# Late modulation vectors as VectorE dot products over transposed w_mod columns, and a second full set of gate and up weight buffers, in an adaLN attention and SwiGLU block

## The chip, the cores and the metric

The kernel runs on one core of one Trainium2 chip. The metric is the device time of one execution in microseconds (us). A time here is the median of several executions. The profile is one execution, and its span (first to last instruction) is about 2 us shorter than the time of the same execution.

The names of the engines: PE is TensorE (matmuls), DVE is VectorE, ACT is ScalarE, POOL is GpSimd, SP is SyncE, which here only issues DMA. "SPq" in a line of the profile is SP's instruction queue.

## The reference

```python
mod = (silu(c) @ w_mod).reshape(1, 6, 1, 1024)       # c: 1 x 1024, w_mod: 1024 x 6144
sa, ca, ga, sb, cb, gb = (mod[:, i] for i in range(6))
h = layernorm(x) * (1 + ca) + sa                     # x: 2048 x 1024
x = x + ga * attention(h)     # 32 heads of 128, 4 KV heads, the last W = 512 of 2048 cached keys
h = layernorm(x) * (1 + cb) + sb
x = x + gb * ffn(h)           # silu(h @ w_gate) * (h @ w_up) @ w_down, width 3584
return x                      # all in bf16
```

The six modulation vectors of 1024 values come from one product of a vector with a matrix. Two of them (sa, ca) are needed at once. The other four are late: the gate ga is first needed when the first chunk of 512 tokens finishes attention, cb and sb when its second layernorm begins, and gb only in the feed-forward part.

## The kernel before

The kernel handles four chunks of 512 tokens. Attention is cut into 128 steps, one head of one chunk each. A step issues 4 score matmuls, 8 matmuls that make q for three steps ahead, from step 13 on 8 matmuls with wo, and 16 matmuls of probabilities with V. By the trace a step takes 3.50 us up to step 12 and 5.22 us from step 13 on, and nearly all of that is PE time. Other work is hung on the steps by `at(k, function, ...)`. After attention comes the feed-forward part (FFN) for all four chunks.

Three parts matter. First, nearly all loads go through one queue, that of SP. While the attention steps are emitted they are pinned in program order, so a load that waits for something holds up every load behind it:

```python
stage = {"dma": True, "steps": False}
def pin(ins, what="steps"):
    return tc.keep_in_program_order(ins) if stage[what] else ins
def fetch(out, in_):
    pin(nc.sync.dma_start(out=out, in_=in_), "dma")
def load_wq(cc, hg, parts=(0, 1)):                    # wq of four heads, in two halves
    for i in parts:
        t = blkB("wq", [P, 4, 512])
        load(t, wq_v[:, 4 * i:4 * i + 4, hg * 512:(hg + 1) * 512])     # load() is a fetch()
        wq_tiles[(cc, hg, i)] = t
...
for k in range(NU + 1):                               # the 128 attention steps
    if k % 4 >= 2 and 4 * (k // 4) + 8 < NU:
        g = 4 * (k // 4) + 8
        load_wq(g // H, (g % H) // 4, (k % 4 - 2,))   # e.g. steps 10, 11: wq first used in step 13
    if k < NU: emit_s(k)
    if k + LEAD < NU: emit_q(k + LEAD)                # LEAD = 3
    run_tasks(k)
    if k >= 1: emit_o(k - 1)
```

Second, the four late vectors. They are made as rows by matmuls with silu(c) as the stationary operand, stored to DRAM as rows, and come back: a gate as a broadcast to all 128 partitions, a column (cb, sb) by a gather of 4-byte values:

```python
def load_rows(vec, part):                             # 1 MB of w_mod, half of one vector's rows
    t = hpool.tile([P, 4, D], BF16, name="wmr", tag="hT")
    load(t, wm_v[:, 4 * part:4 * part + 4, vec * D:(vec + 1) * D])
def mod_rows(n, part):                                # 16 matmuls, four times
    ps = mm("row_ps")
    ...
    nc.tensor.matmul(ps[32 * i:32 * i + 32, :], lhsT=sil32[:, 4 * part + k, :], rhs=..., ...)
    ...
    fetch(out=row_d[n], in_=r[0:P:32, :])             # four rows of 512 fp32
def load_gate(n, k, dst):
    fetch(out=dst..., in_=row_d[n][k:k + 2, :].partition_broadcast(P))
def load_cols(n, k, dst, add_one):
    fetch(out=dst, in_=row_d[n][k:k + 2, :].rearrange("a (b p) -> p (a b)", p=P))
for n, vecs in enumerate(((2, 4), (5, 3))):           # (ga, cb) and (gb, sb)
    for part in range(2):
        k = 16 * n + 8 * part
        at(k, load_rows, vecs[0], part); at(k + 2, load_rows, vecs[1], part)
        at(k + 5, mod_rows, n, part)                  # steps 5, 13, 21, 29
    at(16 * n + 15, load_gate, n, 0, gb_bc if n else ga_bc)
    at(16 * n + 16, load_cols, n, 2, sb if n else cb1, n == 0)
```

Third, the weights of the FFN. Gate and up weights of four 128-wide feature tiles take four buffers of 512 KB. The pool `blkB` has seven, so two full sets (eight) do not fit:

```python
def load_gu(cc, fg):
    for nm, v in (("wg", wg_v), ("wu", wu_v)):
        for i in range(2):
            t = blkB(nm, [P, 4, 512])                 # pool blkB: bufs=7
            load(t, v[:, 4 * i:4 * i + 4, fg * 512:(fg + 1) * 512])
            gu_w[(cc, fg, nm, i)] = t
```

## Time and profile before

| what | before |
|---|---|
| time, median of the first 3 runs | 1285.66 us |
| span of the profiled execution | 1282.7 us |
| PE busy | 1269.7 us (99%) |
| DVE busy | 577.8 us (45%) |
| mean granted TensorE clock | 0.998 |

The first part of the page of the kernel before gives the span and, for each engine, busy time, share and number of instructions:

```profile
span 1282.7 us, 18139 instructions
...
PE 1269.7 (99%) x7601; PEld 642.9 (50%) x7601; DVE 577.8 (45%) x1271; ACT 333.9 (26%) x433; POOL 1.2 (0%) x8
```

PE is the limit: it has 13 us without work in the whole execution. What the change takes away has to be PE work, or one of these few holes. The groups view of the kernel before, restricted to the tile row_ps, shows the PE work in question. Its columns are line, engine, operation, tiles, shape, count, then busy us and mean ns of one, then idle before it:

```profile
L779 PE MATMUL row_ps<-wmr,sil 128*32 128x512 bf16 x64 | 4.2, 382 | 0.0
```

So 64 matmuls take 4.2 us of PE. The waits view of the kernel before shows the holes. A line names who waited, for what, the us in total, how often, and the longest. Here are two waits of PE:

```profile
PE gu_ps L1168 <- DMA wu<-in_B_w_up_dram: 2.1, 1, 2.1
...
PE a_ps L1096 <- DVE acc L1102: 0.7, 1, 0.7
```

And one of DVE, from the same view of that engine:

```profile
DVE modT L802 <- DMA modT<-row_d: 3.4, 1, 3.4
```

The second and the third line belong together: DVE stood 3.4 us on the columns gathered from row_d, an accumulator copy came late behind it, and PE lost 0.7 us. The first line is the only weight wait of the FFN. The timeline of SP around it shows its reason (start, duration, queue, line, operation, tiles, count):

```profile
743.56 6.84 SPq L848 DMA_TRANSPOSE hT<-xn  x4
750.50 0.53 SPq L664 DMA_DIRECT2D wu<-in_B_w_up_dram  x1
```

The timeline of PE shows its end; the square brackets hold the idle time before the instruction and what ended it:

```profile
754.79 1.04 PE L1168 MATMUL gu_ps<-hT,wu 128*128 128x512 bf16 x4 [2.10 <-DMA wu<-in_B_w_up_dram]
```

The wu tile could be issued only at 750.50 us, because its buffer came free late and four transposes, 6.84 us together, stood before it in the queue.

### The profile page before, as it was taken

To read this page: it belongs to the slowest core of one execution; us is meant where nothing else is said; L and a number is where in the kernel's file an instruction comes from. 1 tells how busy PE (TensorE), PEld (TensorE's weight loads), DVE (VectorE), ACT (ScalarE), POOL (GpSimd) and SP (SyncE) were. 2 spreads that over 40 slices of the span, in tenths; PEclk is the share of its full clock that TensorE was granted. 3 is DMA by queue.
4 is the path that set the end of the run, shared out by engine and by line. 5 is a ranking of instruction groups with operands and counts; after the bars stand their busy time and mean duration, and the time that the engine had idled before them with its cause. 6 is when DMAs were issued, how large, how long until landed. Compare 5 with 4: busy or idle time off the path is not lost.

```text
span 1282.7 us, 18139 instructions
## 1 busy us (share of the span) xinstructions
PE 1269.7 (99%) x7601; PEld 642.9 (50%) x7601; DVE 577.8 (45%) x1271; ACT 333.9 (26%) x433; POOL 1.2 (0%) x8
## 2 busy tenths in 40 slices
PE   8999999999999999999999999999999999999998
PEld 4555555555555555555554444444444444444444
DVE  4464467865577755576653642221212221221122
ACT  3543334333333433333341111011100111011100
POOL 0000000000000000000000000000000000000000
PEclk9999999999999999999999999999999999999999
DMA  9888476557355654445487484454536455454401
GB/s 293 269 204 232 152 154 167 141 149 195 91 129 155 144 148 140 123 142 131 132 207 221 142 234 150 140 189 147 181 102 216 143 165 164 135 193 134 146 21 48
DMA packets 280108, 204.21 MB, mean 159 GB/s; under 512 B 113865, under 2 KB 273609, under 8 KB 280018
## 3 DMA queue, kind: packets, MB, share of 16 engines
q1 hardware_dynamic: 275106, 198.78, 54.2%
q10 hardware_dynamic: 4912, 4.20, 1.0%
q8 instruction: 61, 1.00, 0.3%
q14 instruction: 29, 0.24, 0.1%
HBM read 174.08 MB, written 4.21 MB: 139 GB/s over the span
## 4 chain that ended last, share of the span: by engine, by line
PE 95%; DMA 2%; DVE 1%; SPq 1%; ACT 0%; issue 0%; DVEq 0%
PE gu_ps L1168 29%; PE a_ps L1096 17%; PE q_ps L1019 17%; PE d_ps L1188 15%; PE o_ps L1064 9%; PE s_ps L1032 8%; DMA wm<-in_w_mod_dram 1%; SPq L664 1%; DMA hT<-xn 0%; DMA modT<-row_d 0%; DMA wu<-in_B_w_up_dram 0%; PE row_ps L779 0%; PE q_ps L940 0%; DVE st L816 0%; SPq L848 0%; ACT pT L1034 0%
## 5 line engine op out<-in xcount | busy, mean ns | idle before, releaser
L1034 ACT ACTIVATE pT<-s_ps 128x1024 bf16<-128x1024 f32 x256 | 248.7, 1020 | 341.8 <-PE s_ps L1032 341.8
L1096 PE MATMUL a_ps<-wo,oT 128*128 128x512 bf16 x1024 | 241.9, 379 | 0.7 <-DVE acc L1102 0.7
L1019 PE MATMUL q_ps<-hT,wq 128*128 128x512 bf16 x1000 | 236.7, 379 | 0.3 <-DVE modT L755 0.3
L1168 PE MATMUL gu_ps<-hT,wu 128*128 128x512 bf16 x896 | 211.8, 379 | 2.1 <-DMA wu<-in_B_w_up_dram 2.1
L1168 PE MATMUL gu_ps<-hT,wg 128*128 128x512 bf16 x896 | 211.7, 379 | 0.0
L1174 DVE TENSOR_TENSOR guT<-gu_ps,sg 128x512 bf16<-128x512 f32 x112 | 77.4, 691 | 283.5 <-ACT sg L1173 283.5
L1173 ACT ACTIVATE sg<-gu_ps 128x512 bf16<-128x512 f32 x112 | 66.9, 597 | 490.9 <-PE gu_ps L1168 439.7
L1188 PE MATMUL d_ps<-wd,guT 128*128 128x512 bf16 (+2 forms) x952 | 194.2, 366 | 0.0
L916 DVE CAST qT<-q_ps 128x512 bf16<-128x512 f32 x128 | 88.3, 691 | 176.6 <-PE q_ps L1019 176.0
L1096 PEld LDWEIGHTS <-oT 128*128 128x128 bf16 x1024 | 99.9, 98 | 122.1 <-issue 1.9
L1019 PEld LDWEIGHTS <-wq 128*128 128x128 bf16 x1000 | 97.8, 98 | 117.8 <-issue 0.3
L1188 PEld LDWEIGHTS <-guT 128*128 128x128 bf16 x952 | 90.9, 98 | 102.9
L1064 PEld LDWEIGHTS <-pT 128*128 128x128 bf16 x2048 | 126.6, 98 | 30.6 <-issue 0.4
L1168 PEld LDWEIGHTS <-wu 128*128 128x128 bf16 x896 | 87.6, 98 | 108.1 <-DMA wu<-in_B_w_up_dram 2.6
L1168 PEld LDWEIGHTS <-wg 128*128 128x128 bf16 x896 | 87.7, 98 | 105.4
L1064 PE MATMUL o_ps<-v_sb,pT 128*128 128x130 bf16 x2048 | 137.1, 220 | 0.0
L1032 PE MATMUL s_ps<-qT,kT 128*128 128x512 bf16 x512 | 131.5, 379 | 0.6 <-ACT pT L1034 0.6
L1051 DVE TENSOR_TENSOR oq<-o_ps,rl 128x256 bf16<-128x256 f32 (+2 forms) x256 | 101.3, 420 | 4.3
L1192 DVE TENSOR_TENSOR f<-d_ps,gb_bc 128x512 f32<-128x512 f32 (+2 forms) x34 | 22.5, 661 | 147.0 <-PE d_ps L1188 147.0
L1104 DVE TENSOR_TENSOR acc<-a_ps,acc 128x512 f32<-128x512 f32 x64 | 44.1, 689 | 38.9 <-PE a_ps L1096 38.9
L1032 PEld LDWEIGHTS <-kT 128*128 128x128 bf16 x512 | 44.9, 98 | 31.7 <-issue 1.3
L816 DVE BATCH_NORM_STATS2 st<-x 128x6 f32<-128x512 bf16 x64 | 41.3, 680 | 2.9 <-DMA x<-in_A_x_dram 2.6
(75 smaller groups left out, 309.3 us busy)
## 6 DMA issues: line engine op xcount, KB each, us to landing
wq<-in_A_wq_dram SPq DMA_DIRECT2D x64, 512.0 KB, 4.1
wo<-in_A_wo_dram SPq DMA_DIRECT2D x64, 512.0 KB, 5.5
wg<-in_B_w_gate_dram SPq DMA_DIRECT2D x56, 512.0 KB, 5.1
wu<-in_B_w_up_dram SPq DMA_DIRECT2D x56, 512.0 KB, 3.8
wd<-in_B_w_down_dram SPq DMA_DIRECT2D x56, 512.0 KB, 6.4
wmr<-in_w_mod_dram SPq DMA_DIRECT2D x8, 1024.0 KB, 11.4
x<-in_A_x_dram SPq DMA_DIRECT2D x16, 256.0 KB, 5.7
wm<-in_w_mod_dram SPq DMA_DIRECT2D x4, 1024.0 KB, 10.5
```

The lines of the kernel that those rows point to most:

```text
L916: nc.vector.tensor_copy(out=t, in_=q_ps)
L1019: nc.tensor.matmul(q_ps, lhsT=wq_tiles[(cc, h // 4, dt // 4)][:, dt % 4, (h % 4) * P:(h % 4 + 1) * P], rhs=hT[("h1", cc)][:, dt, :], start ...
L1032: nc.tensor.matmul(s_ps[:, i, :], lhsT=kT[:, kv, j * P:(j + 1) * P], rhs=qT[g], start=True, stop=True)
L1034: nc.scalar.activation(out=p[:, 2 * jj:2 * jj + 2, :], in_=s_ps, func=ACT.Exp, scale=scale)
L1051: nc.vector.tensor_tensor(out=dst, in0=ps[:, s0:s0 + cnt, 0:Dh], in1=sc, op=ALU.mult)
L1064: nc.tensor.matmul(o_slot["ps"][:, s_, :], lhsT=pT[g][:, j, t * P:(t + 1) * P], rhs=v_sb[:, kv, j, 0:VN], start=(j == 0), stop=(j == WT - 1))
L1096: nc.tensor.matmul(a_ps, lhsT=oT[(cc, 2 * q + i)][:, hh % 4, t * P:(t + 1) * P], rhs=wo_tiles[(cc, q, dh, i)][:, hh % 4, :], start=(hh == ...
L1104: nc.vector.tensor_tensor(out=acc[(cc, t)][:, dsl], in0=a_ps, in1=acc[(cc, t)][:, dsl], op=ALU.add)
L1168: nc.tensor.matmul(ps[:, n, :], lhsT=gu_w[(cc, fg, nm, dt // 4)][:, dt % 4, fi * P:(fi + 1) * P], rhs=hT[("h2", cc)][:, dt, :], start=(dt ...
L1173: nc.scalar.activation(out=g, in_=ps[:, 0, :], func=ACT.Silu)
L1174: nc.vector.tensor_tensor(out=guT[(cc, fg)][:, fi, :], in0=ps[:, 1, :], in1=g, op=ALU.mult)
L1188: nc.tensor.matmul(d_ps, lhsT=guT[(cc, f // 4)][:, f % 4, t * P:(t + 1) * P], rhs=wd_tiles[(cc, dh, f // 4)][:, f % 4, c0:c0 + w], start=( ...
```

## The change

The intent is threefold. The four late vectors should cost PE nothing: w_mod is loaded transposed by DMA, so that a column of w_mod lies along the free axis of a partition, and DVE multiplies it with silu(c) (broadcast to all partitions) and sums. The result is a column, so cb and sb need no way through DRAM at all. Only the gates, which are needed as rows, go from columns to DRAM and back as a broadcast. And the eighth buffer for gate and up weights is put where V was, which is dead once attention is over.

```diff
-    def load_rows(vec, part): ...      # plain load, 1 MB
-    def mod_rows(n, part): ...         # 16 TensorE matmuls, rows to DRAM
-    def load_cols(n, k, dst, add_one): ...   # columns gathered from DRAM
+    def spread_c():
+        fetch(out=c_d, in_=sil_r)
+        fetch(out=c_bc.rearrange("p (a b) -> p a b", a=DT), in_=c_d.partition_broadcast(P))
+    def load_wmT(vec, part):
+        t = hpool.tile([P, 4, D], BF16, name="wmT", tag="hT")
+        for i in range(4):
+            c0 = vec * D + (4 * part + i) * P
+            pin(nc.sync.dma_start_transpose(out=t[:, i, :], in_=w_mod[:, c0:c0 + P]), "dma")
+    def mod_dot(vec, j, dst):
+        pin(nc.vector.scalar_tensor_tensor(out=junk, in0=t[:, j % 4, :], scalar=1.0, in1=c_bc,
+                                           op0=ALU.mult, op1=ALU.mult, accum_out=dst[:, j:j + 1]))
+    def store_gate(n):
+        d = dp.tile([DT, P], FP32, name="col_d", tag="col_d", bufs=2)
+        with nc.allow_non_contiguous_dma(reason="columns to 1024 values"):
+            fetch(out=d.rearrange("a p -> p a"), in_=mod_col[:, n, :])
+    def load_gate(n, dst):
+        fetch(out=dst.rearrange("p (a b) -> p a b", a=DT), in_=col_d[n].partition_broadcast(P))
 ...
+    at(0, spread_c)
+    for i, (vec, dst) in enumerate(((2, mod_col[:, 0, :]), (4, cb1), (3, sb), (5, mod_col[:, 1, :]))):
+        for part in range(2):
+            k = 1 + 8 * i + 4 * part
+            at(k, load_wmT, vec, part)
+            for j in range(4):
+                at(k + 3 + j, mod_dot, vec, 4 * part + j, dst)
+        k = 1 + 8 * i + 10
+        if vec == 4: at(k, add_one, cb1)
+        elif vec in (2, 5):
+            at(k + 1, store_gate, vec // 5)
+            at(k + 2, load_gate, vec // 5, gb_bc if vec == 5 else ga_bc)
 ...
+    v_blk = v_flat[:, 0:2048].rearrange("p (a b) -> p a b", a=4)          # in V's place
     def load_gu(cc, fg):
         for nm, v in (("wg", wg_v), ("wu", wu_v)):
             for i in range(2):
-                t = blkB(nm, [P, 4, 512])
+                spare = (cc * NFG + fg) % 2 == 1 and nm == "wu" and i == 1
+                t = v_blk if spare else blkB(nm, [P, 4, 512])
```

More of the change, by code (lines that the diff above doesn't have):

```diff
@@ L756, in mod_cols @@
                                 scalar1=1.0 if add_one else 0.0, scalar2=None, op0=ALU.add)
-    sil32 = const.tile([P, DT, 32], BF16, name="sil32")
-    for dt in range(DT):
-        nc.vector.tensor_scalar(out=sil32[:, dt, :], in0=ones_bf[:, 0:32],
-                                scalar1=siluc[:, dt:dt + 1], scalar2=None, op0=ALU.mult)
-    wm_rows = []
-    row_part = []
-    row_d = {}
-    def load_rows(vec, part):
-        t = hpool.tile([P, 4, D], BF16, name="wmr", tag="hT")
-        load(t, wm_v[:, 4 * part:4 * part + 4, vec * D:(vec + 1) * D])
-        wm_rows.append(t)
@@ L774, in mod_rows @@
-    def mod_rows(n, part):
-        ps = mm("row_ps")
-        tiles = [wm_rows.pop(0) for _ in range(2)]
-        for k in range(4):
-            for i in range(4):
-                nc.tensor.matmul(ps[32 * i:32 * i + 32, :], lhsT=sil32[:, 4 * part + k, :],
-                                 rhs=tiles[i // 2][:, k, (i % 2) * 512:(i % 2 + 1) * 512],
-                                 start=(k == 0), stop=(k == 3))
-        if part == 0:
-            r = blkC("row", [P, TCW], FP32)
-            nc.vector.tensor_copy(out=r, in_=ps)
-            row_part.append(r)
-        else:
-            r = row_part.pop()
-            nc.vector.tensor_tensor(out=r, in0=ps, in1=r, op=ALU.add)
-            d = dp.tile([4, TCW], FP32, name="row_d", tag="row_d", bufs=2)
-            fetch(out=d, in_=r[0:P:32, :])
-            row_d[n] = d
@@ L793, in load_gate @@
-    def load_gate(n, k, dst):
-        fetch(out=dst.rearrange("p (a b) -> p a b", a=2),
-                          in_=row_d[n][k:k + 2, :].partition_broadcast(P))
-    def load_cols(n, k, dst, add_one):
-        src = row_d[n][k:k + 2, :].rearrange("a (b p) -> p (a b)", p=P)
-        with nc.allow_non_contiguous_dma(reason="1024 values to columns"):
-            fetch(out=dst, in_=src)
-        if add_one:
-            nc.vector.tensor_scalar(out=dst, in0=dst, scalar1=1.0, scalar2=None, op0=ALU.add)
+    c_d = dp.tile([DT, P], BF16, name="c_d", tag="c_d", bufs=1)
@@ new lines, in fast_path @@
+    c_bc = const.tile([P, D], BF16, name="c_bc")
+    mod_col = const.tile([P, 2, DT], FP32, name="mod_col")
+    wm_cols = {}
+    col_d = {}
+    def spread_c():
[6 more added lines that the diff above has]
+            pin(nc.sync.dma_start_transpose(out=t[:, i, :], in_=w_mod[:, c0:c0 + P]), "dma")
+        wm_cols[(vec, part)] = t
@@ new lines, in mod_dot, with add_one @@
+    def mod_dot(vec, j, dst):
+        t = wm_cols[(vec, j // 4)]
+        junk = wk.tile([P, D], BF16, name="junk", tag="junk", bufs=1)
+        pin(nc.vector.scalar_tensor_tensor(out=junk, in0=t[:, j % 4, :], scalar=1.0, in1=c_bc,
+                                           op0=ALU.mult, op1=ALU.mult,
+                                           accum_out=dst[:, j:j + 1]))
+    def add_one(dst):
+        pin(nc.vector.tensor_scalar(out=dst, in0=dst, scalar1=1.0, scalar2=None, op0=ALU.add))
+    def store_gate(n):
+        d = dp.tile([DT, P], FP32, name="col_d", tag="col_d", bufs=2)
+        with nc.allow_non_contiguous_dma(reason="columns to 1024 values"):
+            fetch(out=d.rearrange("a p -> p a"), in_=mod_col[:, n, :])
+        col_d[n] = d
@@ L1111, in emit_wo @@
             nc.vector.tensor_tensor(out=x1, in0=f, in1=x1, op=ALU.add)
-    for n, vecs in enumerate(((2, 4), (5, 3))):
+    at(0, spread_c)
+    for i, (vec, dst) in enumerate(((2, mod_col[:, 0, :]), (4, cb1), (3, sb),
+                                    (5, mod_col[:, 1, :]))):
         for part in range(2):
-            k = 16 * n + 8 * part
-            at(k, load_rows, vecs[0], part)
-            at(k + 2, load_rows, vecs[1], part)
-            at(k + 5, mod_rows, n, part)
-        at(16 * n + 15, load_gate, n, 0, gb_bc if n else ga_bc)
-        at(16 * n + 16, load_cols, n, 2, sb if n else cb1, n == 0)
+            k = 1 + 8 * i + 4 * part
[3 more added lines that the diff above has]
+        k = 1 + 8 * i + 10
+        if vec == 4:
+            at(k, add_one, cb1)
+        elif vec in (2, 5):
+            at(k + 1, store_gate, vec // 5)
+            at(k + 2, load_gate, vec // 5, gb_bc if vec == 5 else ga_bc)
     for tt in range(QT, S // P):
@@ L1152, in fast_path @@
     wd_tiles = {}
+    v_flat = v_sb.rearrange("p a b c -> p (a b c)")
+    v_blk = v_flat[:, 0:2048].rearrange("p (a b) -> p a b", a=4)
     def load_gu(cc, fg):
```

## The prediction

> **What bounds the kernel now.** TensorE: the page shows PE busy 1269.7 of 1282.7 us (99%), clock 0.998. About half of the idle 13 us is the start, where the chain of waits ends on the first w_mod loads until 22 us; nothing changes there. DVE is busy 45%. So the change can only win TensorE time and the few holes in it.
>
> **What it removes, all on the critical path.**
> 1. The 64 row_ps matmuls: four bursts, 4.2 us busy (groups view); a step with a burst takes 4.58 instead of 3.50 us (timeline, score matmuls). -4.2 us.
> 2. The DVE wait for the columns loaded from row_d (waits view, 3.4 us), which held an accumulator copy back and left PE idle 0.73 us (step 6.12 instead of 5.22 us). They now come by a DVE sum. -0.8 us.
> 3. The hole at 752.7-754.8 us: gu_ps waited 2.1 us for a wu tile, issued only at 750.5 behind four hT transposes, because with seven buffers the eighth tile waits until its predecessor group is nearly done. With the spare buffer it goes out some 18 us earlier. -2.2 us. It is the only FFN weight wait in the waits view, so the second full set wins no more.
>
> Sum: -7.2 us.
>
> **What it adds.**
> - 32 dot products of 128x1024 on DVE. The same form (squares of wq) takes 1.215 us plus 0.08 us for the accumulator: about 40 us, in steps 4 to 36 (42 to 195 us). DVE is busy about 2 us per 3.5-us step there; a dot raises that to 3.0-3.2, and in steps 10-12, where layernorm adds about 1 us, over 3.5. From step 13 a step is 5.2 us. DVE runs in order and may free PSUM late: 1 to 3 us of PE idle in steps 8-16.
> - 32 DMA transposes of 256 KB for 8 plain loads of 1 MB. SyncE spends 1.25 us issuing an hT transpose, 0.5 us on a plain megabyte: 5 us per half vector, not 0.5. Four hT transposes moved 220 GB/s in their best 2 us (stretches view), plain loads 350. The Trainium skill ("DMA: Bandwidth & Descriptors", Latency and other measured facts) gives 261 GB/s, near this. So 2-3.5 us more DMA time per half, where the DMA share is already 0.8-1.0 up to 128 us, and the one in-order queue also carries wq, wo and oT. Followed step by step, wq still lands 2-5 us before its use: 0 to 2 us lost, before 110 us.
> - c through DRAM and column stores of 4-byte elements (about 5 us to land, like modT): hidden.
>
> **Prediction.** -7.2 + 2.5 = -4.7 us: 1281.0 us, 8 times in 10 between 1275.5 and 1290.0. Faster by over 2%: 0.01; within 2%: 0.95; slower by over 2%: 0.04.
>
> **What would show it.** Right: no row_ps; no gu_ps wait for wu; PE busy about 1265.5; FFN stages unchanged otherwise; DVE busy about 612 us, dots near 1.22 us; new PE idle only between 40 and 130 us, released by DVE (qT, oq, acc) or by wq or wo DMA. Wrong: PE idle after 200 us, or a wu wait elsewhere.
>
> **What would make it wrong.** Transposes straight from w_mod (256-byte rows, 12-KB pitch) far slower than those from SBUF, so that dots block DVE and DVE blocks PSUM by several us per half; or the SP queue falling behind, which adds up before step 13: then 15-30 us slower. If DVE absorbs the dots wholly: 1278.

## More of the kernel before

One more view of the kernel before is needed later, the timeline of SP in the early steps. It shows when wq was issued, and what stood before it:

```profile
51.61 0.81 SPq L664 DMA_DIRECT2D wq<-in_A_wq_dram  x1
52.52 1.31 SPq L664 DMA_DIRECT2D wmr<-in_w_mod_dram  x1
58.46 6.15 SPq L1081 DMA_TRANSPOSE oT<-oq  x4
64.66 0.58 SPq L664 DMA_DIRECT2D wq<-in_A_wq_dram  x1
...
77.40 0.45 SPq L664 DMA_DIRECT2D wq<-in_A_wq_dram  x1
...
84.50 0.53 SPq L664 DMA_DIRECT2D wq<-in_A_wq_dram  x1
```

The issues at 51.61 and 64.66 us are the two halves of the wq that step 13 uses first (step 13 began at 72.32 us), those at 77.40 and 84.50 us are for step 17 (it began at 95.19 us). One load of a megabyte of w_mod, at 52.52 us, holds the queue for 1.31 us. The queue runs 8 to 11 us ahead of the use.

## The result, and the profile after

| | before | after |
|---|---|---|
| time, median of the fast runs of the same rounds (6 each) | 1286.62 us | 1293.48 us |
| range | 1285.42 to 1288.03 | 1289.08 to 1294.75 |
| span of the profiled execution | 1282.7 us | 1291.7 us |
| PE busy | 1269.7 us | 1270.2 us |
| DVE busy | 577.8 us | 606.9 us |
| mean granted clock | 0.998 | 0.992 |

The ratio is 1.005, with a 95% interval of 1.0034 to 1.0066. A ratio here is the mean time of one kernel's fast runs over that of the other's of the same rounds, so it is not quite the ratio of the medians. The kernel became slower by 0.5%. That is within 2%, but it is outside the predicted range of 1275.5 to 1290.0 us, and the sign is wrong.

The first part of the page after:

```profile
span 1291.7 us, 18094 instructions
...
PE 1270.2 (98%) x7537; PEld 641.9 (50%) x7537; DVE 606.9 (47%) x1323; ACT 333.8 (26%) x433; POOL 1.2 (0%) x8
```

PE has 64 matmuls fewer and yet is busy 0.5 us longer, and its idle time grew from 13 to 21.5 us. The parts of the change that were meant to gain are there. There is no group row_ps, no wait of PE for wu and no wait of DVE for modT. The groups view of the kernel after shows the spare buffer in use (224 matmuls read their up weights from V's place) and the dots with the duration that was foreseen:

```profile
L1174 PE MATMUL gu_ps<-hT,v_sb 128*128 128x512 bf16 x224 | 57.5, 379 | 0.0
```

```profile
L783 DVE SCALAR_TENSOR_TENSOR junk<-wmT,c_bc 128x1024 bf16<-128x1024 bf16 x32 | 38.9, 1215 | 0.0
```

What is new is in the waits view of PE after. One line there has no counterpart before:

```profile
PE q_ps L1014 <- DMA wq<-in_A_wq_dram: 9.2, 3, 3.6
```

The timeline of PE after places its three waits, one in step 13 and two in step 17:

```profile
77.18 1.48 PE L1014 MATMUL q_ps<-hT,wq 128*128 128x512 bf16 x4 [3.01 <-DMA wq<-in_A_wq_dram]
```

```profile
101.68 1.89 PE L1014 MATMUL q_ps<-hT,wq 128*128 128x512 bf16 x4 [2.61 <-DMA wq<-in_A_wq_dram]
107.17 1.89 PE L1014 MATMUL q_ps<-hT,wq 128*128 128x512 bf16 x4 [3.60 <-DMA wq<-in_A_wq_dram]
```

The waits view of SP's queue between 24 and 112 us, after, shows where the queue itself stood still:

```profile
SPq L664 <- DMA col_d<-mod_col: 7.2, 1, 7.2
SPq L664 <- DMA c_d<-sil_r: 4.8, 1, 4.8
```

The timeline of SP after answers to the lines shown of before:

```profile
39.80 9.16 SPq L777 DMA_TRANSPOSE wmT<-in_w_mod_dram  x4
...
57.19 9.09 SPq L777 DMA_TRANSPOSE wmT<-in_w_mod_dram  x4
...
67.00 0.45 SPq L664 DMA_DIRECT2D wq<-in_A_wq_dram  x1
67.55 5.63 SPq L1076 DMA_TRANSPOSE oT<-oq  x4
73.27 0.53 SPq L664 DMA_DIRECT2D wq<-in_A_wq_dram  x1
73.90 0.46 SPq L664 DMA_DIRECT2D col_d<-mod_col  x1
...
76.98 0.57 SPq L664 DMA_DIRECT2D wo<-in_A_wo_dram  x1
84.78 0.34 SPq L664 DMA_DIRECT2D ga_bc<-col_d  x1
85.17 9.25 SPq L777 DMA_TRANSPOSE wmT<-in_w_mod_dram  x4
...
95.33 0.44 SPq L664 DMA_DIRECT2D wq<-in_A_wq_dram  x1
...
102.99 0.53 SPq L664 DMA_DIRECT2D wq<-in_A_wq_dram  x1
```

Two things are to be seen. First, three of the first four groups of four transposes of w_mod columns hold the queue for 9.1 to 9.3 us (the very first, at 31.87 us, for 5.62 us), where a plain megabyte before held it for 1.31 us. So the second half of the wq for step 13 goes out at 73.27 us instead of 64.66 us. Step 13 had come to it at 74.2 us, and PE went on only at 77.2 us. Second, the store of the gate's columns goes out at 73.90 us, and the broadcast load that needs it, ga_bc, can be issued only at 84.78 us: the wait of 7.2 us in the view above. Behind it stand the next four transposes, and behind those the wq for step 17, at 95.33 and 102.99 us instead of 77.40 and 84.50 us.

In the DMA view of the kernel after, cut to 74 to 86 us, each of the 40 columns is 0.3 us. The first line is the mean busy share of the 16 DMA engines in tenths, the second what they moved in GB/s:

```profile
DMA  9293899999999000000000042376220230432029
GB/s 256 40 113 89 317 365 365 346 129 153 250 261 197 14 14 0 0 0 0 0 0 0 0 51 79 48 48 31 20 41 10 7 17 7 31 44 48 27 31 85
```

Just before 78 us the rate falls to 14 GB/s, then to nothing for 2.4 us, and then it is 7 to 85 GB/s up to 86 us, though the load of wo issued at 76.98 us was waiting. ("Standstill" below means this stretch of almost no data moved.) Over the 4 KB of the store alone a line of the list of issues (tiles, count, KB each, median us from issue to landing) says 10.8 us:

```profile
col_d<-mod_col SPq DMA_DIRECT2D x2, 4.0 KB, 10.8
```

The second store of this kind in the changed kernel, at 206.68 us, is followed by 22 GB/s from 210 to 217 us and holds the queue for 8.7 us, but there PE lost nothing.

The windows view adds the clock. Its columns are the stretch, its length, busy time of PE, PEld, DVE, ACT and POOL with the number of instructions, the granted clock (PEclk), the DMA share and GB/s. Before, in the stretches of the two losses:

```profile
72.30:82.40 10.10, 10.10 (x72) 4.87 (x71) 6.09 (x14) 4.15 (x6) 0.00 (x0) 1.00 0.57 161
98.00:113.00 15.00, 15.00 (x106) 8.29 (x105) 6.75 (x17) 5.81 (x6) 0.00 (x0) 1.00 1.15 293
```

After:

```profile
72.30:82.40 10.10, 7.09 (x40) 3.22 (x38) 6.09 (x14) 2.44 (x4) 0.00 (x0) 0.83 0.64 128
98.00:113.00 15.00, 8.79 (x41) 3.49 (x39) 5.45 (x15) 2.21 (x4) 0.00 (x0) 0.66 1.18 235
```

The waits of PE in the second stretch sum to 6.2 us. A mean clock of 0.66 over the same 15 us means that about 10 us of it ran at half clock.

Step by step, the 9.0 us between the spans divide like this. A step is timed from the start of its first exponential on ACT (tile pT), 0.6 us after its first score matmul in both traces:

| part | us |
|---|---|
| start, up to the first step (28.77 instead of 27.09 us) | +1.7 |
| bursts of row_ps gone from steps 5, 13, 21, 29 (6.31 or 4.58 us, now 5.22 or 3.50) | -4.3 |
| columns no longer gathered (step 16: 6.11, now 5.23) | -0.9 |
| step 13: 10.09 us where 5.22 is usual | +4.9 |
| step 17: 14.88 us where 5.22 is usual | +9.7 |
| dots in steps 33 to 35 | +0.3 |
| from step 127 to the end (614.2, now 611.9 us) | -2.3 |

The sum is +9.1 us. So the gain of about 7.5 us came, and 14.6 us were lost in two steps. This is one execution of each kernel, and the start varies between executions (see the last experiment). In the view of SP's queue above stands also a wait of 4.8 us for c_d, at 26 to 31 us; the runs with plain loads and with the later vectors keep that store and lose nothing in step 13, so it does not cause that loss alone.

### The profile page after: what moved, and what is told of

Same layout as the page of the kernel before. It is cut to its first block, busy times and chain, and to the rows that moved or that the text cites. A ratio compares the mean times of both kernels' runs of the same rounds, so it can differ in the third digit from the quotient of the medians.

```text
span 1291.7 us, 18094 instructions
## 1 busy us (share of the span) xinstructions
PE 1270.2 (98%) x7537; PEld 641.9 (50%) x7537; DVE 606.9 (47%) x1323; ACT 333.8 (26%) x433; POOL 1.2 (0%) x8
## 4 chain that ended last, share of the span: by engine, by line
PE 96%; DMA 2%; DVE 1%; SPq 1%; issue 0%; ACT 0%
PE gu_ps L1174 30%; PE a_ps L1091 17%; PE q_ps L1014 17%; PE d_ps L1194 15%; PE o_ps L1059 9%; PE s_ps L1027 8%; DMA wm<-in_w_mod_dram 1%; DMA wq<-in_A_wq_dram 1%; SPq L664 1%; PE q_ps L935 0%; DVE junk L950 0%; DVE junk L783 0%; DVE qT L911 0%; ACT pT L1029 0%; DVE oq L1046 0%
## 5 line engine op out<-in xcount | busy, mean ns | idle before, releaser
L1014 PE MATMUL q_ps<-hT,wq 128*128 128x512 bf16 x1000 | 239.6, 382 | 9.5 <-DMA wq<-in_A_wq_dram 9.2
L1091 PE MATMUL a_ps<-wo,oT 128*128 128x512 bf16 x1024 | 244.6, 382 | 0.0
L1174 PE MATMUL gu_ps<-hT,wu 128*128 128x512 bf16 x672 | 163.3, 379 | 0.0
L1174 PEld LDWEIGHTS <-wu 128*128 128x128 bf16 x672 | 65.7, 98 | 79.3
L1174 PE MATMUL gu_ps<-hT,v_sb 128*128 128x512 bf16 x224 | 57.5, 379 | 0.0
```

Source lines behind the costliest of these rows:

```text
L1014: nc.tensor.matmul(q_ps, lhsT=wq_tiles[(cc, h // 4, dt // 4)][:, dt % 4, (h % 4) * P:(h % 4 + 1) * P], rhs=hT[("h1", cc)][:, dt, :], start ...
L1091: nc.tensor.matmul(a_ps, lhsT=oT[(cc, 2 * q + i)][:, hh % 4, t * P:(t + 1) * P], rhs=wo_tiles[(cc, q, dh, i)][:, hh % 4, :], start=(hh == ...
L1174: nc.tensor.matmul(ps[:, n, :], lhsT=gu_w[(cc, fg, nm, dt // 4)][:, dt % 4, fi * P:(fi + 1) * P], rhs=hT[("h2", cc)][:, dt, :], start=(dt ...
```

## The experiments

Theory A says that the whole loss comes through the one in-order queue: the transposes hold it too long, and the store of 1024 single values stops it and what it feeds. Theory C says that DVE, with 32 dots of 1.215 us in the early steps, frees PSUM and makes oq late, so that transposes and loads start late. Theory B, in one of the expectations, is that the DMA time of the transposes alone does it. A smaller question is the share of the changed start. Ratios below are against runs of the kernel before on the same chip in the same rounds (its medians there: 1285.64 us for the first four, 1285.79 for the next four, 1285.65 for the last three).

### The spare buffer alone

To the kernel before only the buffer in V's place is added.

```diff
-                t = blkB(nm, [P, 4, 512])
+                spare = (cc * NFG + fg) % 2 == 1 and nm == "wu" and i == 1
+                t = v_blk if spare else blkB(nm, [P, 4, 512])
```

> The kernel before with only the spare buffer in V's place; the w_mod rows stay on TensorE. If the hole at 752.7-754.8 us is all that the second full set is worth: 2.2 us faster than the kernel before, no gu_ps wait for wu, attention unchanged. Rival (the spare's loads, which queue behind V's last reader, hold other loads up): no gain or a loss, with new gaps after 670 us.

Measured: 1284.18 us, ratio 0.9986 (0.9970 to 1.0003). The profile has no wait for wu. It has a new wait of 0.8 us of the gate and up matmuls for DVE, so this hole shrank by 1.3 us instead of 2.1, and this execution's start was 1.0 us longer, although the start was not changed. The same wait for DVE (0.6 to 1.3 us) is in the profiles of five more runs with the spare buffer. The median agrees with the expected gain, but the interval includes 1, so a gain in time is not shown by this run alone.

### The gate loaded eight steps later

```diff
-            at(k + 2, load_gate, vec // 5, gb_bc if vec == 5 else ga_bc)
+            at(k + 10, load_gate, vec // 5, gb_bc if vec == 5 else ga_bc)
```

> The changed kernel with the two gate loads eight steps later, so that the queue need not stand still until the column store has landed (7.2 us at 77-85 us in its trace). Theory A (the in-order queue falls behind, and the wait for the store is the largest part): the loss of 9.7 us in step 17 shrinks to under 3 us, the loss of 4.9 us in step 13, which comes before the store, stays; 1284 to 1287 us. Theory B (the transposes' DMA time alone): step 17 stays near 14.9 us and the total above 1291 us. Theory C (DVE dots): the same as B.

Measured: 1291.3 us, ratio 1.0038 (1.0021 to 1.0054). This missed the 1284 to 1287 us of theory A. SP's queue no longer waited for col_d. But the DMA engines stood still all the same: 61 GB/s from 78 to 82 us and 32 GB/s from 82 to 86 us. The four transposes issued in that time took 14.35 us of the queue instead of 9.25. The step times were 12.23 us in step 13 (10.09 in the changed kernel) and 11.17 us in step 17. The total is that of theory B, but step 17 is not, as B expected, still near 14.9 us. So theory A in its first form was too narrow. Most of the cost is not the wait for the store but the store itself: almost nothing behind it moves for some 8 us.

### Plain loads in the transposes' place (wrong result)

The same tiles are filled by one plain load of 1 MB, so the dots compute with wrong numbers (relative error 0.17). Nothing else changes.

```diff
-        for i in range(4):
-            c0 = vec * D + (4 * part + i) * P
-            pin(nc.sync.dma_start_transpose(out=t[:, i, :], in_=w_mod[:, c0:c0 + P]), "dma")
+        load(t, wm_v[:, 4 * part:4 * part + 4, vec * D:(vec + 1) * D])
```

> The changed kernel with one plain load of 1 MB of w_mod rows in place of each four transposes; the dots run on the same tiles, so the result is wrong on purpose. Theory A: the queue is 5 to 9 us per half vector less behind, step 13 loses nothing, and step 17 loses under 3 us although the wait for the store is still there; 1279 to 1284 us. Theory C (DVE dots late): the stalls stay, 1290 us or more.

Measured: 1286.41 us, ratio 0.9998 (0.9981 to 1.0014). The loss of step 13 was gone, so the transposes are its cause, by the queue or by the DMA engines (the run with wq on another queue, below, separates the two). The loss of step 17 stayed at 7.4 us, with a wait for wq of 4.8 us and two waits of the queue for col_d of 18.1 us together. The expected 1279 to 1284 us were missed for that reason: the store of columns was still there.

### No dots (wrong result)

Each dot is replaced by a copy of one column (relative error 0.19).

```diff
-        pin(nc.vector.scalar_tensor_tensor(out=junk, in0=t[:, j % 4, :], scalar=1.0, in1=c_bc, ...))
+        pin(nc.vector.tensor_copy(out=dst[:, j:j + 1], in_=t[:, j % 4, 0:1]))
```

> The changed kernel with each dot product replaced by a copy of one column (wrong result on purpose); transposes, stores and gate loads stay. Theory A and B: the stalls at steps 13 and 17 stay, 1290 to 1294 us. Theory C (DVE full with dots frees PSUM and oq late, and so delays the queue): they go, 1279 to 1282 us.

Measured: 1292.57 us, ratio 1.0053 (1.0036 to 1.0070), the same as with the dots. PE waited 9.8 us for wq, and steps 13 and 17 lost 4.3 and 9.5 us. Only the 0.3 us of steps 33 to 35 were gone. Theory C falls.

### The gate stored as rows

The gate's column block (128 x 8) is cast to bf16, transposed by one TensorE instruction and stored as 8 rows of 512 bytes. The result is correct.

```diff
+        nc.vector.tensor_copy(out=gate_b, in_=mod_col[:, n, :])          # to bf16
+        nc.tensor.transpose(ps, gate_b, ident)
+        nc.vector.tensor_copy(out=gate_r, in_=ps)                        # 8 x 128, fp32
-        fetch(out=d.rearrange("a p -> p a"), in_=mod_col[:, n, :])
+        fetch(out=d, in_=gate_r)
```

> The changed kernel with the gate columns turned into rows on TensorE (one 128x8 transpose each, two small DVE copies) and stored as 8 rows of 512 bytes instead of 1024 single values; schedule, transposes and dots as in the changed kernel. If the store of single values stops the DMA engines for some 8 us (they moved 2 to 41 GB/s from 78 to 86 us): the store lands within 4 us, the stretch from 78 to 86 us moves over 150 GB/s, and the loss in step 17 falls from 9.7 to under 3 us; step 13 keeps its 3 to 6 us; 1284 to 1288 us. Rival (the transposes alone keep the queue behind): step 17 still takes over 11 us, 1290 us or more.

Measured: 1283.68 us, ratio 0.9976 (0.9961 to 0.9992). Step 17 took 5.22 us: its loss was gone. The same cut of the DMA view as above, 74 to 86 us, now in this run:

```profile
GB/s 115 229 352 358 365 333 228 179 113 246 231 207 157 280 348 352 410 434 437 382 317 283 200 213 279 290 288 243 89 60 230 251 248 159 129 113 79 20 9 226
```

The standstill is gone as well. The store was issued at 73.32 us and the load that needs it at 76.99 us, so it took at most 3.7 us. What stayed is a loss of 6.4 us in steps 12 and 13 of the profiled execution, with a wait for wq of 2.9 us and two low quanta of the clock (a quantum is 3.4 us at half clock, the unit in which these traces show it). That is the part that the transposes make. Its size is that of one execution: the profiled one was the slowest of the four (1285.05 us at a mean clock of 0.995; the others took 1281.32 to 1284.64 us at 0.999 to 1.000).

### The late vectors twelve steps later

```diff
-            k = 1 + 8 * i + 4 * part
+            k = 13 + 8 * i + 4 * part
```

(The same for the second `k`.) The transposes then fall in steps of 5.22 us with wo instead of those of 3.50 us, where loads are densest.

> The changed kernel with the whole modulation work 12 steps later (first transposes in step 13 instead of 1), where a step takes 5.2 us instead of 3.5. Theory A (the queue only lacks time in the short steps): steps 13 and 17 lose nothing, the 8 us of the column store find slack, 1278 to 1282 us. Rival (the transposes and stores cost about the same wherever they are): the losses move to steps 25 to 45, 1288 us or more. A third possibility is DVE, which then has the dots beside the squares of wq in steps 32 to 45: PE idle released by DVE there, 1 to 4 us.

Measured: 1284.82 us, ratio 0.9992 (0.9977 to 1.0008). Steps 13 and 17 lost nothing. But the store took its loss elsewhere: the queue waited twice for col_d, 19.1 us together, the following loads came late, and step 29 took 10.03 us. The timeline of SP and that of PE in this run:

```profile
129.83 0.43 SPq L664 DMA_DIRECT2D wo<-in_A_wo_dram  x1
141.04 0.34 SPq L664 DMA_DIRECT2D ga_bc<-col_d  x1
```

```profile
160.73 1.89 PE L1014 MATMUL q_ps<-hT,wq 128*128 128x512 bf16 x4 [3.35 <-DMA wq<-in_A_wq_dram]
```

So the expected 1278 to 1282 us were missed, and so was the rival's 1288 us or more. Moving the work cures the loss of step 13, but not the store.

### Both: rows, and twelve steps later

> Row store and later schedule together. If each removes its own part: no PE wait for wq at all, only the start and noise are left, 1278 to 1281 us, 5 to 8 us faster than the kernel before.

Measured: 1281.53 us over 5 rounds, ratio 0.9966 (0.9952 to 0.9979), correct. PE waits for neither wq nor wo. Left are 0.3 us in steps 24 and 25, 0.2 in step 29, 0.3 in steps 33 and 34 and about 1.4 in steps 45 to 49; what makes them was not tested. The expected 1278 to 1281 us, 5 to 8 us faster, were just missed: it is 4.3 us faster. With both causes taken away, the predicted gain is seen in the time. That the net is close to the predicted -4.7 us is partly luck: the costs that are left are the start and these small losses, not those that the prediction added up.

### Stores alone, in the kernel before

To the kernel before, which has none of the rest, three stores of 4 KB are added whose result nobody reads: two with the access pattern of the column store (steps 27 and 92), and between them one of 32 bytes per partition, contiguous in DRAM (step 60).

```diff
+            fetch(out=d, in_=ca1)                          # step 60: 128 pieces of 32 bytes
+            fetch(out=d.rearrange("a p -> p a"), in_=ca1)  # steps 27, 92: 1024 values of 4 bytes
```

> The kernel before with three extra stores that nothing reads: the 1024 single values of one 128x8 tile at steps 27 and 92, and the same tile as 128 pieces of 32 bytes at step 60. If single values are what costs: the two column stores land in 8 to 11 us and the DMA engines move under 50 GB/s meanwhile, the 32-byte store lands in under 4 us. If the long landing in the changed kernel came from the traffic around it: the column stores land in under 5 us here, where the queue is emptier.

Measured: 1284.93 us, one look without a state. The first column store, at 145.09 us, had one load of wo behind it: 37 GB/s from 150 to 155 us, where in the kernel before the same load was through by 148 us and nothing moved after it. The second was issued at 480.45 us, between two halves of wq and two loads of wo, and the store of pieces at 313.62 us in the same company. The DMA view of this run, 480 to 492 us, again 0.3 us for a column of the first line; the second line is from the list of issues (count, KB each, median us to landing):

```profile
GB/s 218 77 0 126 133 270 362 362 325 146 26 25 126 266 11 24 3 14 14 14 0 68 51 61 24 3 27 51 58 34 24 17 34 24 34 17 31 20 20 27
...
wq<-in_A_wq_dram SPq DMA_DIRECT2D x2, 512.0 KB, 14.5
```

For comparison the kernel before with the same loads, without a store, 479 to 491 us:

```profile
GB/s 212 84 0 113 154 314 369 375 324 178 130 164 218 307 338 379 335 335 369 328 362 362 396 382 382 212 102 34 24 7 0 0 0 0 0 0 0 0 0 0
```

And around the store of pieces, 313 to 325 us:

```profile
GB/s 219 185 70 0 58 287 358 375 386 239 70 46 72 246 324 352 348 362 389 389 362 348 382 379 365 358 294 120 31 24 24 17 0 0 0 0 27 0 0 0
...
wq<-in_A_wq_dram SPq DMA_DIRECT2D x2, 512.0 KB, 3.9
```

After the column store the engines fall to 0 to 68 GB/s from 484 us to the end of the window, with loads outstanding: wq took 14.5 us to land. Without a store the same loads were through in about 8 us, and with the store of pieces as well (3.9 us for wq). PE lost nothing in this place, at full clock: the queue was far enough ahead. When the stores themselves landed is not on record in this run, so that part of the expectation was not tested. So the standstill belongs to the store, and the loss to the standstill meeting a queue without slack. Why single values stop the engines is not shown. These runs separate a store of 1024 pieces of 4 bytes from one of 128 pieces of 32 bytes, not the size of a piece from the number of pieces. The packet records add one thing: in the changed kernel 1019 packets of 4 bytes start within 1 us, from 76 to 77 us, and the standstill comes after them.

### wq through another engine's queue

In the changed kernel wq is issued by GpSimd during the attention steps, so that it need not stand behind the store and the transposes.

```diff
+            nc.gpsimd.dma_start(out=t, in_=wq_v[:, 4 * i:4 * i + 4, hg * 512:(hg + 1) * 512])
-            load(t, wq_v[:, 4 * i:4 * i + 4, hg * 512:(hg + 1) * 512])
```

> The changed kernel with the wq loads of the attention steps issued by GpSimd instead of SyncE, so that they no longer stand behind the transposes and the store wait in one queue; the DMA engines are the same. If the in-order queue is what makes wq late: no wait for wq in step 13, and step 17 loses only what the stopped engines cost, under 5 us; 1280 to 1285 us. If the DMA engines' time is what is short (transposes at about 200 GB/s, 8 us of standstill): wq is late all the same, 1289 us or more. A third outcome is a new wait, if GpSimd's issues are slow.

Measured: 1297.39 us, ratio 1.0089 (1.0069 to 1.0109), slower than the changed kernel. The waits view of PE in this run:

```profile
PE a_ps L1095 <- DMA wo<-in_A_wo_dram: 6.8, 1, 6.8
...
PE q_ps L1018 <- DMA wq<-in_A_wq_dram: 1.9, 1, 1.9
```

Step 13 lost nothing (5.22 us), though the transposes were still there: what made wq late in step 13 was its place in SP's queue behind them. The wait for wq fell from 9.2 to 1.9 us, all of it in step 1. But wo, still behind the store in SP's queue, took its place with 6.8 us in step 17. After the store little moved, as before (29 GB/s from 80 to 84 us). So the expected 1280 to 1285 us were missed; 1289 us or more came, but by the wait for wo and not by a late wq, as that outcome had it. The Trainium skill ("DMA: Bandwidth & Descriptors", Issuing engines are not separate DMA queues) says that DMAs of all issuing engines end up on the same 16 DMA engines, and this trace agrees: two loads of wq that GpSimd issued at 75.71 and 76.57 us, beside the store, landed after 13.2 and 18.0 us, the two before them after 4.6 and 8.8 us. The other queue also brought losses of its own: +3.7 us in step 1 (the wait for wq, then a low clock) and +4.2 us in step 22 (a wait of 2.4 us for DVE, then a low clock).

### The order of the start

In six of the profiles with the changed start (after, the runs with plain loads, with rows and with the later vectors, and the two runs with both cures and no further change) a stretch of half clock begins at 21 to 24 us. It lasts 3.4 us, or twice that (one quantum or two). In the profiles with the old start (before, the spare buffer alone, the stores alone, and the first run of this section) one begins at 12.8 to 15.0 us. The rule is not strict: two profiles with the changed start have none there, and that with wq on the other queue has one at 14.0 us. The two without began their first score matmul at 26.31 and 26.15 us, no later than the kernel before (26.46 us). The version with both cures was given eight dead DVE instructions (they write into c_bc before it is loaded), so that the scheduler emits the start in the old order again.

```diff
+    sil32 = c_bc[:, 0:256].rearrange("p (a b) -> p a b", a=DT)
+    for dt in range(DT):
+        nc.vector.tensor_scalar(out=sil32[:, dt, :], in0=ones_bf[:, 0:32], ...)
```

> Row store and later schedule as in e7, plus the eight small DVE operations that the change removed, put back as dead work, because they make the scheduler emit the start in the old order (the second 32 modulation matmuls before the last transposes). If the old order is what keeps TensorE's clock up when the last w_mod tile arrives at 21 us: no low-clock quantum between 20 and 28 us, first score matmul at 26.1 to 27.0 us instead of 27.6, and a median 0.7 to 1.5 us under e7's. If the quantum falls by chance: no difference from e7 in the medians.

> e7's kernel again, on the same chip and in the same rounds as e10, for the comparison: 1280 to 1283 us.

Measured, 5 rounds each with the same runs of before: 1280.71 us with the old start order, ratio 0.9958 (0.9944 to 0.9971); 1282.19 us without, ratio 0.9964 (0.9950 to 0.9979). In the windows view of the run with the old order the low clock is seen early:

```profile
12.00:16.00 4.00, 2.17 (x41) 1.99 (x43) 0.63 (x2) 1.28 (x3) 0.00 (x0) 0.60 1.09 348
...
24.00:28.00 4.00, 3.95 (x19) 1.74 (x19) 2.17 (x5) 1.27 (x2) 0.00 (x0) 1.00 0.88 222
```

and in that of the run without it, late:

```profile
12.00:16.00 4.00, 2.88 (x53) 2.07 (x53) 0.98 (x3) 0.98 (x2) 0.00 (x0) 1.00 1.09 348
...
24.00:28.00 4.00, 4.00 (x11) 1.44 (x10) 0.54 (x1) 0.53 (x1) 0.00 (x0) 0.50 0.87 208
```

The means differ by 1.1 us (1280.75 and 1281.82), about two standard errors. The profile does not show the early start that was expected: the first score matmul comes at 27.74 us instead of 26.1 to 27.0 (27.64 us in the first run with both cures, 29.26 us in the one of the same rounds). That the changed order costs something at the start (+1.7 us in the accounting) is thus possible and not settled. The version with both cures and the old start is the fastest measured, about 5 us below the kernel before.

## Why the prediction was wrong

**Right: what is won on PE.** Predicted were -4.2 us for the row_ps matmuls, -0.8 us for the wait behind modT and -2.2 us for the wu hole. The traces show -4.3, -0.9 and -2.3 us. The run with the spare buffer alone gained less in its own profile (1.3 us in the FFN), because a wait for DVE took part of it. As predicted, the new idle time of PE after the start lies between 40 and 130 us (74 to 107 us) and ends with a load of wq.

**Right: the cost of a dot.** 1.215 us each was predicted and measured, and DVE is busy 606.9 us (predicted about 612). What the dots cost PE was overrated: 1 to 3 us predicted, about 0.3 us in the trace, gone in the run without dots.

**Wrong, step 1: "Followed step by step, wq still lands 2-5 us before its use: 0 to 2 us lost, before 110 us."** The term was mis-sized at its root. A group of four transposes was put at 5 us of the queue, from the 1.25 us of an hT transpose. The first group came near that (5.6 us), the next three held it for 9.1 to 9.3 us. The Trainium skill ("DMA: Bandwidth & Descriptors", Latency and other measured facts) gives 261 GB/s for DMA transposes; the stretches view shows 174 GB/s from 44 to 50 us and 219 from 57 to 66 us, with everything else that moved then included, so the page's figure was not reached here. The issue alone does not take 9.1 us: the same four transposes took 5.3 to 6.1 us in three groups of this trace, 6.26 us in the fourth group of the run with rows, and 14.35 us beside the column store. So something beside the issue adds to it; what, is not shown. wq landed about 3 us too late in step 13 instead of 2 to 5 us early. The run with plain loads removed exactly this loss, and so did the run that took wq out of the queue behind the transposes.

**Wrong, step 2: "column stores of 4-byte elements (about 5 us to land, like modT): hidden."** This is the larger part. The gather of modT reads single values, the new store writes them. The one was taken for the other, and they are not alike: the gather landed in 5.1 us (the second one, at 172.1 us; for the first no landing is on record), the store was 10.8 us under way, and the DMA engines moved next to nothing for most of that. The number of packets does not make the difference: the gather's 4-byte packets (978 of them start from 88 to 90 us in the kernel before) are followed by 354 GB/s from 90 to 93 us, the store's by 2 GB/s from 78 to 80 us. Replacing it by rows of 512 bytes removed the loss of step 17, and adding it to the kernel before reproduced the standstill. The Trainium skill ("DMA: Bandwidth & Descriptors", Specifications) says that below 512 bytes a DMA engine does a read-modify-write. The store of single values fits this in direction, but the store in 32-byte pieces, also below that size, showed no standstill, so it is not shown to be the cause. The same page (Rules for kernel authors) says that a non-contiguous last dimension "Lowers to one descriptor per element" and to rearrange it. The trace agrees: the DMA records of the changed kernel hold 14,034 packets of 4 bytes, those of the run with rows 11,970, which is about 1032 fewer for each of the two stores. The prediction had read past that rule.

**Missing from the sum: the clock.** A stall of PE is not paid once. In step 17 the waits are 6.2 us and the loss is 9.7 us, in step 13 they are 3.0 and 4.9 us. The difference is half-clock time, PEclk 0.66 and 0.83 in the windows. It can also explain why PE was busy for 1270.2 us and not for the predicted 1265.5 us: in the two steps PE worked for some 10 us at half clock, about 5 us more than at full clock (an estimate from the windows). The Trainium skill ("TensorE: Matmul & The Clock Gate", What's actually happening) says that the clock falls to half after an idle window of about 3.4 us. In the trace of the changed kernel low-clock quanta of 3.4 us begin within 0.5 us of the end of waits of 2.6 and 3.0 us, so a wait a little shorter than the window was enough. After the wait of 2.1 us in the kernel before there is none, but after one of 1.9 us in the run with wq on another queue there is, so the length alone does not decide.

**The warning named in the prediction** ("Transposes straight from w_mod ... far slower", "or the SP queue falling behind, which adds up before step 13: then 15-30 us slower") had the right place for one of the two losses. It was given too small a chance, and its size was smaller: 4.9 us in step 13.

**Not settled.** Why a store of 1024 single values stops the engines, what limits the transposes when they are slow, and how much of the 1.7 us at the start is the order of its instructions.

## What to carry to other kernels

When loads share one in-order queue, cost a new DMA by how long it holds the queue and the DMA engines, not by its bytes, and compare that with how far ahead the queue runs at the place where it is put: here 8 to 11 us of lead were eaten by transposes of 9.2 us and a 4-KB store of 10.8 us. Do not store single values to DRAM from a column across partitions: a small transpose on TensorE and a store of 512-byte rows turned a loss of 0.5% into a gain of 0.2%, and of 0.3% with the work placed later. And count more for a PE stall than its length: here the clock fell after those of about 3 us, and the step lost about half as much again (4.9 us for a wait of 3.0, 9.7 for 6.2, 4.8 for 3.35).

## What the Trainium skill lacked or had wrong

- "DMA: Bandwidth & Descriptors" advises against a non-contiguous last dimension, but does not say what a store of 1024 single 4-byte values costs, nor that it holds up the other DMAs of its core. The runs show 10.8 us from issue to landing for 4 KB, 2 GB/s moved by all engines from 78 to 80 us and 20 to 41 GB/s up to 86 us, reproduced with the store alone in the kernel before (0 to 68 GB/s for some 8 us, a load of wq 14.5 us under way). The same 4 KB in 128 pieces of 32 bytes left the loads behind it at 246 to 389 GB/s, and wq landed in 3.9 us.
- The limit of 512 bytes in "DMA: Bandwidth & Descriptors" does not by itself say which small stores hurt: 128 pieces of 32 bytes and 1024 of 4 bytes are both below it, and only the second store stopped the engines.
- "DMA: Bandwidth & Descriptors" gives a bandwidth for DMA transposes, and issuing times only in a comparison made for trn3; how long transposes like these hold the queue on this chip it does not say. The traces show 5.3 to 9.3 us for four of 128 x 1024 straight from w_mod in the changed kernel, and 14.35 us beside the column store.
- "TensorE: Matmul & The Clock Gate" puts the drop of the clock at an idle window of about 3.4 us. Here waits of 2.6 and 3.0 us, and one of 2.4 us in the run without dots, were also followed by quanta at half clock (PEclk 0.50 from 78 to 80 us after a wait of 3.0 us).
